# Attention followed by a gated MLP on one core: score visits in pairs over two PSUM tiles, the values of all heads in one tile, and a third PSUM bank for H

## The chip, the cores and the metric

The kernel runs on one core of one Trainium2 chip. The metric is the device time of one execution in microseconds (us); less is better. A core has a matmul engine (TensorE, PE in the profile, with its weight loads shown apart as PEld), a vector engine (DVE), an activation engine (ACT), GpSimd (POOL) and a queue engine (SP) that issues transfers. Matmuls write to PSUM, which has eight banks of 512 fp32 columns for each of 128 partitions; ACT and DVE read it.

## The reference

The inputs are q, k, v of 8 batches, 8 heads, 576 positions, 64 channels, and the weights of an MLP. Cut to what matters:

```python
scores = scale * q @ k.T                       # per batch and head, 576 x 576
rel = pos[:, None] - pos[None, :]
scores = where((rel >= 0) & (rel < 128), scores - slope[head] * abs(rel), -1e9)
attn = softmax(scores)                         # so each row sees at most 128 keys
x = (attn @ v)  as [8 * 576 tokens, 512]
h = x @ w_in                                   # 512 -> 2048
g = h * sigmoid(beta * h)
out = g @ w_out                                # 2048 -> 512, fp32
```

## The kernel before, in words

A batch has 5 blocks of queries (four of 128 rows, one of 64). Because of the window, a block of 128 keys is seen only by its own and the next block of queries. Scores are computed transposed: keys on the partitions, queries along the columns.

**Attention of batches 2 to 7.** A *score visit* is SC (L391): for one pair of heads p and one half m of a batch it makes 4 (m=0) or 6 (m=1) matmuls into the tile SS, which has two banks, one for each head of the pair. Each matmul contracts over 64 channels only, so it uses one half of the array's rows; the two heads of a pair (e = 0, 1) lie in the two halves. Then ACT takes Exp of all 1024 columns to the SBUF tile pt (L411), and DVE multiplies pt by the decay and the mask in one table (factor, L158 and L163). A batch has 4 pairs times 2 halves, 8 visits; batches 2 to 7 have 48. PV (L423) multiplies the weights of a block with v, for four heads g in one bank of the pool psum_t (two banks); a column of ones in v gives the sum of the weights. norm (L325) takes the reciprocal on DVE (L327) and multiplies (L328) into xn. Batches 0 and 1 have functions of their own (SP_, PVP, XP), which the change leaves as they are.

**Transposition.** X (L447) brings xn into XT, with the 512 channels on the partitions: for batches 2 and 3 with four TensorE transposes into a psum_t bank and a copy on DVE (L466); for batches 4 to 7 (XDMA = 4) with a transposing DMA from the SP queue (L455).

**MLP.** The 4608 tokens form nine groups g of 512 (NTG). Hm/HS (L475) makes one of 16 tiles of H: four matmuls of 512 columns into a bank of psum_h (two banks, named hps), then ACT takes Tanh (sig, L495; with half of beta, so that it serves as the sigmoid), then DVE makes gT from sig and hps (L496). OS (L505) makes a quarter n of an output tile i: four matmuls (L514) into a bank of psum_o (two banks, tag "ops"); after the last quarter the tile is halved to osb, by DVE for groups 0 and 1 (L522) and by ACT from group 2 on (L524), and stored. In groups 1 and 2 every second H tile up to a point (FOUR) also takes a bank of psum_o. The opening uses a tile SX of two banks; when it is closed, psum_o takes its place (open_o, L745).

**Loads.** q, k and v of the next batch come in blocks by DMAs of the SP queue (get, L188), are cast to bf16 on POOL (cast_qk, cast_v), and q and k are transposed by DMAs of the SP queue too (DT, L378).

**Order.** TensorE, SP and POOL keep the order in which the program lists the steps (manual_schedule, L598), each its own. The lists att (attention of batches 2 to 7) and items (H and O of a group) are merged: SC steps with the PV and X steps of the half before (merged, pvx, L547), the loads of batch b+1 at fixed places among the steps of batch b (jobs, L536), and spread (L715) puts the att steps between the items of a group by their weights, so that a group's tokens are ready before its first H. Each group g starts with H(g,0), needs the X blocks of its tokens, and ends with the output tiles O(g,0) and O(g,1), 32 matmuls without H between them; O(g,2) and O(g,3) fall among the H of the next group.

```python
for g in range(2, NTG):
    h = HG(g)
    o = (OG(g - 1, 2) if g > 2 else []) + OG(g - 1, 3)
    ...
    items += OG(g, 0) + OG(g, 1)
```

Of the kernel before, what the change touches and what calls it, by code (L numbers as in the profile page):

```python
# [19 lines left out]
def kernel(  # L20
# [62 lines left out]
    osb_pool = ctx.enter_context(tc.tile_pool(name="osb", bufs=4))  # L83
    psum_c = ctx.enter_context(tc.tile_pool(name="psum_c", bufs=1, space=bass.MemoryType.PSUM))
    psum_h = ctx.enter_context(tc.tile_pool(name="psum_h", bufs=2, space=bass.MemoryType.PSUM))
    psum_t = ctx.enter_context(tc.tile_pool(name="psum_t", bufs=2, space=bass.MemoryType.PSUM))
    SS = psum_c.tile([P, 2, 512], F32, name="SS")
    psum_c.seal()
    opening = ExitStack()
    psum_x = opening.enter_context(tc.tile_pool(name="psum_x", bufs=1, space=bass.MemoryType.PSUM))  # L90
    SX = psum_x.tile([P, 2, 512], F32, name="SX")
    late, gates = {}, {}

    def after(ins, other):
        tc.add_manual_dep(
# [219 lines left out]
    def room(b, shape):  # L315

        if b == 0:
            return psum_h.tile(shape, F32, name="pvh", tag="hps")[:]
        if "o" in late:
            return late["o"].tile(shape, F32, name="pvo", tag="ops")[:]  # L320
# [67 lines left out]

    COLS = {0: (0, 384), 1: (128, 256), 2: (0, 384), 3: (192, 320), 4: (128, None)}

    def SC(b, m, p):  # L391
        assert all((b, sb) in moved for sb in range((3, 5)[m]))
        qk = QK[b % 2]
        for kb in ((0, 1), (2, 4, 3))[m]:
            at, then = COLS[kb]
            nq = {3: P + 64, 4: 64}.get(kb, 2 * P)
            for e in range(2):
                o = SS[:, e, at : at + min(nq, 512 - at)]
                if kb in (0, 2):
                    o = bass.AP(  # L400
                        tensor=o.tensor, offset=o.offset,
                        ap=[list(o.ap[0]), [then - at, 2], [1, P]],
                    )
                nc.tensor.matmul(  # L404
                    o,
                    lhsT=qk[64 * e : 64 * e + 64, 1, p, P * kb : P * kb + P],
                    rhs=qk[64 * e : 64 * e + 64, 0, p, P * kb : P * kb + nq],
                    start=True, stop=True, skip_group_check=True,
                )
        pt = pt_pool.tile([P, 2, 512], BF16, name="pt", tag="pt")  # L410
        nc.scalar.activation(out=pt[:], in_=SS[:], func=ACTF.Exp, scale=qscale)  # L411
        factor(pt, m, p)
        pts[b, m, p] = pt

    def weights(b, kb, h, then):
        p, e = divmod(h, 2)
# [6 lines left out]
    def PV(b, qb, g):  # L423
        assert ("v", b, qb) in moved
        nq = ROWS[qb]
        vs = VS[b % 2]
        if g == 0:
            xns[b, qb] = xn_pool.tile([P, H, D], BF16, name="xn", tag="xn")
        xn = xns[b, qb]
        if b:  # L430
            pv = psum_t.tile([P, 4, 66], F32, name="pv", tag="t")
        else:
            pv = late["o"].tile([P, 4, 66], F32, name="pvo", tag="ops")
        for hl in range(4):
            h = 4 * g + hl
            if qb:
                nc.tensor.matmul(  # L437
                    pv[:, hl, 0 : D + 1], lhsT=weights(b, qb - 1, h, 1),
                    rhs=vs[:, qb - 1, h, 0 : D + 1], start=True, stop=False,
                )  # L440
            nc.tensor.matmul(  # L441
                pv[:, hl, 0 : D + 1], lhsT=weights(b, qb, h, 0),
                rhs=vs[:, qb, h, 0 : D + 1], start=qb == 0, stop=True,
            )
        norm(xn[0:nq, 4 * g : 4 * g + 4, :], pv, nq)

    def X(b, qb):  # L447
        nq = ROWS[qb]
        xnv = xns.pop((b, qb))[:].rearrange("p h d -> p (h d)")
        if b >= XDMA:  # L450
            tok0 = (b * S + P * qb) % XTR
            n1 = min(nq, XTR - tok0)
            for r0, r1, at in ((0, n1, tok0), (n1, nq, 0)):
                if r0 < r1:
                    nc.sync.dma_start(  # L455
                        out=XT[:, :, at : at + r1 - r0], in_=xnv[r0:r1], transpose=True)
            return
        xt = psum_t.tile([P, NDM, P], BF16, name="xt", tag="t")
        for c in range(NDM):
            nc.tensor.transpose(  # L460
                out=xt[:, c, 0:nq], in_=xnv[0:nq, c * P : (c + 1) * P],
                identity=ident[0:nq, 0:nq]
            )
        tok0 = (b * S + P * qb) % XTR
        n1 = min(nq, XTR - tok0)
        nc.vector.tensor_copy(out=XT[:, :, tok0 : tok0 + n1], in_=xt[:, :, 0:n1])  # L466
        if n1 < nq:
            nc.vector.tensor_copy(out=XT[:, :, 0 : nq - n1], in_=xt[:, :, n1:nq])
# [6 lines left out]
    def Hm(g, j, cs):  # L475
        if j == 0 and cs[0] == 0:
            gts[g] = gt_pool.tile([P, NFF, TOKG], BF16, name="gT", tag="gT")
        c0 = (g * TOKG) % XTR
        if cs[0] == 0:
            if g == 0 and j in (0, 3):  # L480
                hs[g, j] = SX[:, j // 2]
            elif j % 2 and j < FOUR.get(g, 0):
                hs[g, j] = late["o"].tile([P, DM], F32, name="hpo", tag="ops")[:]
            else:
                hs[g, j] = psum_h.tile([P, TOKG], F32, name="hps", tag="hps")[:]
        hps = hs[g, j]
        for c in cs:
            nc.tensor.matmul(  # L488
                hps, lhsT=W1[:, c, bass.ts(j, P)], rhs=XT[:, c, c0 : c0 + TOKG],
                start=(c == 0), stop=(c == NDM - 1),  # L490
            )
        if cs[-1] < NDM - 1:
            return
        sig = sig_pool.tile([P, TOKG], BF16, name="sig", tag="sig")
        gates[g, j] = nc.scalar.activation(out=sig[:], in_=hps, func=ACTF.Tanh, scale=beta_h[:, j : j + 1])  # L495
        gates["gT"] = nc.vector.scalar_tensor_tensor(  # L496
            out=gts[g][:, j, :], in0=sig[:], scalar=1.0, in1=hps, op0=ALU.add, op1=ALU.mult
        )
# [6 lines left out]
    def OS(g, i, n):  # L505
        gT = gts[g]
        if n == 0:
            late[g, i] = late["o"].tile([P, DM], F32, name="ops", tag="ops")
        ops_ = late[g, i][:]
        last = (g, i) == (NTG - 1, 3)  # L510
        for at in ((0, 256) if last else (0,)):
            cols = slice(at, at + 256) if last else slice(0, DM)
            for j in range(NFF) if last else range(4 * n, 4 * n + 4):
                nc.tensor.matmul(  # L514
                    ops_[:, cols], lhsT=gT[:, j, i * P : i * P + P], rhs=W2[:, j, cols],
                    start=(j == 0), stop=(j == NFF - 1),
                )
# [80 lines left out]
    with tc.manual_schedule(engines={ENG.PE, ENG.SP, ENG.Pool}):  # L598
# [157 lines left out]
        for f in steps:  # L756
# [58 lines left out]
```

## Time and profile before

| what | value |
|---|---|
| time, median of 8 runs | 331.97 us (331.13 to 334.83) |
| the profiled execution's own time | 331.97 us |
| its span (first to last instruction) | 330.2 us |
| granted TensorE clock | 1.00 |
| PE busy | 314.5 us (95%), 2252 matmuls in the records |
| DVE, ACT, POOL busy | 198.3 (60%), 186.6 (57%), 91.0 (28%) us |
| H matmuls L488 on hps | 131.7 us, 379 ns each |
| O matmuls L514 | 136.1 us, 373 ns each |
| Exp of a visit, L411 | x48, 1019 ns each |
| sig L495, gT L496 | 688 ns, 683 ns each |
| norm: reciprocal L327, product L328 | 173 ns, 420 ns each |
| chain that ended last | PE 81%, DMA 5%, DVE 4%, ACT 3%, SP queue 3% |

Busy times of matmuls overlap with each other in the records: a matmul of 512 columns is listed with 379 ns, while four of them start within 0.86 us. So distances are taken between starts. A few per cent of the matmul records are missing; a block of four then shows three. "issue" as a releaser means that nothing in the profile held the instruction back.

### The profile page before, as it was taken

The numbers are of one execution on the slowest core, as the hardware profiler recorded it, in microseconds if no ns is written. First come the engines' busy times: TensorE is split into PE (matmuls) and PEld (weight loads), VectorE is DVE, ScalarE is ACT, GpSimd is POOL, SyncE is SP. The second block draws the span as 40 slices with busy tenths as digits, with TensorE's granted clock in tenths as the row PEclk, the third lists the DMA queues.
The fourth block names the chain that finished last, engine by engine and source line by source line (L and its number), as shares of the span: only waits on it lengthen the run. The fifth ranks groups of instructions, "written<-read, shape, count | busy, mean of one in ns | idle before, by whom it ended". The sixth has DMA issues, their size and how long they took to land.

```text
span 330.2 us, 6005 instructions
## 1 busy us (share of the span) xinstructions
PE 314.5 (95%) x2252; PEld 150.3 (46%) x2294; DVE 198.3 (60%) x424; ACT 186.6 (57%) x265; POOL 91.0 (28%) x150
## 2 busy tenths in 40 slices
PE   7889979999999999999999999999999999999995
PEld 3454544443544454444444444444444445444443
DVE  6687777655669874866278627662877267334500
ACT  6858868615428744676466745664676465345511
POOL 4965811426544342443213221322000000000000
PEclk9999999999999999999999999999999999999999
DMA  7999999999999999999869896997022101210021
GB/s 216 251 256 248 178 197 216 198 191 209 248 186 254 198 205 235 205 187 217 189 124 211 167 231 131 203 190 151 18 64 57 64 16 50 58 64 33 4 94 64
DMA packets 147822, 51.80 MB, mean 157 GB/s; under 512 B 135360, under 2 KB 143824, under 8 KB 147792
## 3 DMA queue, kind: packets, MB, share of 16 engines
q1 hardware_dynamic: 139152, 38.29, 63.8%
q0 software_dynamic: 4864, 6.29, 9.6%
q10 hardware_dynamic: 3776, 6.83, 5.7%
q8 instruction: 18, 0.29, 0.4%
q14 instruction: 12, 0.10, 0.1%
HBM read 36.71 MB, written 9.44 MB: 140 GB/s over the span
## 4 chain that ended last, share of the span: by engine, by line
PE 81%; DMA 5%; DVE 4%; ACT 3%; SPq 3%; issue 2%; POOL 0%; ACTq 0%; DVEq 0%; POOLq 0%
PE ops L514 36%; PE hps L488 31%; DMA fst<-in_k_dram 5%; PE SS L404 4%; PE hpo L488 2%; SPq L205 2%; PE pv L441 2%; PE pv L437 2%; ACT pt L411 2%; DVE gT L496 1%; SPq L194 1%; PE xt L460 1%; ACT sig L495 1%; DVE pt L163 1%; ACT osb L524 1%
## 5 line engine op out<-in xcount | busy, mean ns | idle before, releaser
L514 PE MATMUL ops<-W,gT 128*128 128x512 bf16 (+1 forms) x574 | 136.1, 373 | 1.8 <-issue 0.6
L488 PE MATMUL hps<-XT,W 128*128 128x512 bf16 x511 | 131.7, 379 | 2.3 <-DVE gT L496 1.0
L496 DVE SCALAR_TENSOR_TENSOR gT<-sig,hps 128x512 bf16<-128x512 bf16 x133 | 90.2, 683 | 67.8 <-ACT sig L495 66.7
L495 ACT ACTIVATE sig<-hps,beta_h 128x512 bf16<-128x512 f32 x133 | 91.2, 688 | 61.4 <-PE hps L488 55.3
L514 PEld LDWEIGHTS <-gT 128*128 128x128 bf16 x592 | 54.1, 98 | 58.3 <-issue 3.0
L488 PEld LDWEIGHTS <-W 128*128 128x128 bf16 x576 | 50.5, 97 | 56.6 <-issue 7.1
L411 ACT ACTIVATE pt<-SS 128x1024 bf16<-128x1024 f32 x48 | 48.9, 1019 | 21.0 <-PE SS L404 21.0
L230 POOL CAST vs<-fst 128x512 bf16<-128x512 f32 (+1 forms) x40 | 26.9, 673 | 58.3 <-DMA fst<-in_v_dram 55.9
L524 ACT ACTIVATE osb<-ops 128x512 f32<-128x512 f32 (+1 forms) x28 | 16.5, 589 | 42.9 <-PE ops L514 42.9
L215 POOL CAST bst<-fst 128x512 bf16<-128x512 f32 (+1 forms) x32 | 20.6, 644 | 55.2 <-DMA fst<-in_q_dram 40.7
L328 DVE TENSOR_TENSOR xn<-pv,zs 128x256 bf16<-128x256 f32 (+1 forms) x62 | 26.0, 420 | 1.3
L216 POOL CAST bst<-fst 128x512 bf16<-128x512 f32 (+1 forms) x32 | 20.7, 647 | 19.5 <-DMA fst<-in_k_dram 19.4
L163 DVE TENSOR_TENSOR pt<-pt,fall 128x1024 bf16<-128x1024 bf16 x24 | 19.0, 790 | 10.3 <-ACT pt L411 10.2
L158 DVE TENSOR_TENSOR pt<-pt,falls 128x1024 bf16<-128x1024 bf16 x24 | 17.4, 723 | 12.6 <-ACT pt L411 12.5
L441 PE MATMUL pv<-vs,pt 128*128 128x65 bf16 x240 | 21.6, 193 | 0.0
L441 PEld LDWEIGHTS <-pt 128*128 128x128 bf16 x240 | 16.5, 97 | 8.4
L404 PE MATMUL SS<-qkT 64*128 64x256 bf16 (+2 forms) x240 | 18.9, 252 | 0.6
L437 PE MATMUL pv<-vs,pt 128*128 128x65 bf16 x192 | 18.1, 193 | 0.0
L437 PEld LDWEIGHTS <-pt 128*128 128x128 bf16 x192 | 15.2, 98 | 5.6
L522 DVE TENSOR_SCALAR osb<-ops 128x512 f32<-128x512 f32 (+1 forms) x9 | 5.9, 655 | 19.6 <-PE ops L514 19.6
L404 PEld LDWEIGHTS <-qkT 64*128 64x128 bf16 x240 | 8.0, 94 | 20.5 <-issue 18.6
L327 DVE RECIPROCAL zs<-pv 128x4 f32<-128x4 f32 (+1 forms) x67 | 11.1, 173 | 3.4 <-PE pv L441 2.8
(84 smaller groups left out, 180.6 us busy)
## 6 DMA issues: line engine op xcount, KB each, us to landing
fst<-in_k_dram SPq DMA_DIRECT2D x32, 256.0 KB, 5.4
fst<-in_q_dram SPq DMA_DIRECT2D x32, 256.0 KB, 5.3
fst<-in_v_dram SPq DMA_DIRECT2D x32, 256.0 KB, 4.7
out_dram<-osb ACTq DMA_DIRECT2D x26, 256.0 KB, 2.7
W<-in_moe_w_in_dram POOLq DMA_DIRECT2D x4, 512.0 KB, 7.9
W<-in_moe_w_out_dram POOLq DMA_DIRECT2D x4, 512.0 KB, 12.3
out_dram<-osb POOLq DMA_DIRECT2D x8, 256.0 KB, 4.0
fst<-in_q_dram SPq DMA_DIRECT2D x8, 128.0 KB, 3.9
```

The lines of the kernel that those rows point to most:

```text
L163: nc.vector.tensor_tensor(out=x, in0=x, in1=bass.AP(tensor=t.tensor, offset=t.offset, ap=[list(t.ap[0]), [P, 4], [0, 2], [1, P]]), op=ALU. ...
L216: return nc.gpsimd.tensor_copy(out=t[0:rows, 1], in_=fs.pop(("k", b, sb))[0:rows])
L230: return nc.gpsimd.tensor_copy(out=VS[b % 2][0:rows, sb, :, 0:D], in_=fs.pop(("v", b, sb))[0:rows])
L328: nc.vector.tensor_tensor(out=xn, in0=pv[0:nq, :, 0:D], in1=zs[0:nq].broadcast_to([nq, 4, D]), op=ALU.mult)
L404: nc.tensor.matmul(o, lhsT=qk[64 * e : 64 * e + 64, 1, p, P * kb : P * kb + P], rhs=qk[64 * e : 64 * e + 64, 0, p, P * kb : P * kb + nq], ...
L411: nc.scalar.activation(out=pt[:], in_=SS[:], func=ACTF.Exp, scale=qscale)
L437: nc.tensor.matmul(pv[:, hl, 0 : D + 1], lhsT=weights(b, qb - 1, h, 1), rhs=vs[:, qb - 1, h, 0 : D + 1], start=True, stop=False,)
L441: nc.tensor.matmul(pv[:, hl, 0 : D + 1], lhsT=weights(b, qb, h, 0), rhs=vs[:, qb, h, 0 : D + 1], start=qb == 0, stop=True,)
L488: nc.tensor.matmul(hps, lhsT=W1[:, c, bass.ts(j, P)], rhs=XT[:, c, c0 : c0 + TOKG], start=(c == 0), stop=(c == NDM - 1),)
L495: gates[g, j] = nc.scalar.activation(out=sig[:], in_=hps, func=ACTF.Tanh, scale=beta_h[:, j : j + 1])
L496: gates["gT"] = nc.vector.scalar_tensor_tensor(out=gts[g][:, j, :], in0=sig[:], scalar=1.0, in1=hps, op0=ALU.add, op1=ALU.mult)
L514: nc.tensor.matmul(ops_[:, cols], lhsT=gT[:, j, i * P : i * P + P], rhs=W2[:, j, cols], start=(j == 0), stop=(j == NFF - 1),)
```

## The change

- SC takes two pairs of heads: the matmuls of both come one after the other, the first pair's into one tile, the second's into another, then both Exp and both factors. The second tile is ST, two banks that psum_t held until X(1,4); psum_t is closed there (open_s).
- PV of batches 2 to 7 becomes PVB: one step for all 8 heads of a block, into the two banks of SS or ST, whichever was used longer ago (span), with one reciprocal and one product.
- X of batches 2 and 3 writes to SS or ST too, by matmuls with the identity instead of transposes, in fp32, and the copy to XT moves from DVE to ACT.
- psum_o has two tags of one bank each, "ops" and "h3". Up to group 1 output tiles and the H tiles of FOUR alternate between them. From group 2 on every third H tile (j % 3 == 2) takes "h3", output tiles take "ops", and output tile 0 of a group (and tile 2 of the last) takes a bank of psum_h.
- In att a pair of visits has twice the weight of a visit, PVB that of two PV. So steps stand in another order among the items.

The diff, without what is only renamed for it:

```diff
-    psum_t = ctx.enter_context(tc.tile_pool(name="psum_t", bufs=2, space=bass.MemoryType.PSUM))
+    trans = ExitStack()
+    psum_t = trans.enter_context(tc.tile_pool(side="right", name="psum_t", bufs=2, space=bass.MemoryType.PSUM))
...
+    spans = [SS]
+
+    def span():
+
+        spans.append(spans.pop(0))
+        return spans[-1]
+
+    def obank(name, tag=None):
+        if tag is None:
+            late["n"] = late.get("n", 0) + 1
+            tag = "ops" if late["n"] % 2 else "h3"
+        return late["o"].tile([P, DM], F32, name=name, tag=tag)[:]
...
-    def SC(b, m, p):
+    def SC(b, m, pp):
+
...
-        for kb in ((0, 1), (2, 4, 3))[m]:
-            at, then = COLS[kb]
-            nq = {3: P + 64, 4: 64}.get(kb, 2 * P)
-            for e in range(2):
-                o = SS[:, e, at : at + min(nq, 512 - at)]
...
+        spans.sort(key=lambda t: t is not SS)
+        for p, sps in zip(pp, spans):
+            for kb in ((0, 1), (2, 4, 3))[m]:
+                at, then = COLS[kb]
+                nq = {3: P + 64, 4: 64}.get(kb, 2 * P)
+                for e in range(2):
+                    o = sps[:, e, at : at + min(nq, 512 - at)]
...
-                nc.tensor.matmul(
-                    o,
-                    lhsT=qk[64 * e : 64 * e + 64, 1, p, P * kb : P * kb + P],
-                    rhs=qk[64 * e : 64 * e + 64, 0, p, P * kb : P * kb + nq],
...
-        pt = pt_pool.tile([P, 2, 512], BF16, name="pt", tag="pt")
-        nc.scalar.activation(out=pt[:], in_=SS[:], func=ACTF.Exp, scale=qscale)
-        factor(pt, m, p)
-        pts[b, m, p] = pt
+        for p, sps in zip(pp, spans):
+            pt = pt_pool.tile([P, 2, 512], BF16, name="pt", tag="pt")
+            nc.scalar.activation(out=pt[:], in_=sps[:], func=ACTF.Exp, scale=qscale)
+            factor(pt, m, p)
+            pts[b, m, p] = pt
...
-            pv = late["o"].tile([P, 4, 66], F32, name="pvo", tag="ops")
+            pv = room(1, [P, 4, 66])
...
+    def PVB(b, qb):
+
+        assert ("v", b, qb) in moved
+        nq = ROWS[qb]
+        vs = VS[b % 2]
+        xn = xns[b, qb] = xn_pool.tile([P, H, D], BF16, name="xn", tag="xn")
+        pv = span()[:, :, 0 : 4 * 66].rearrange("p g (h x) -> p g h x", x=66)
+        for h in range(H):
+            o = pv[:, h // 4, h % 4, 0 : D + 1]
+            if qb:
+                nc.tensor.matmul(
+                    o, lhsT=weights(b, qb - 1, h, 1), rhs=vs[:, qb - 1, h, 0 : D + 1],
+                    start=True, stop=False, skip_group_check=True)
+            nc.tensor.matmul(
+                o, lhsT=weights(b, qb, h, 0), rhs=vs[:, qb, h, 0 : D + 1],
+                start=qb == 0, stop=True, skip_group_check=True)
+        zs = xn_pool.tile([P, 2, 4, 1], F32, name="zb", tag="zb")
+        nc.vector.reciprocal(out=zs[0:nq], in_=pv[0:nq, :, :, D : D + 1])
+        nc.vector.tensor_tensor(
+            out=xn[0:nq].rearrange("p (g h) d -> p g h d", g=2), in0=pv[0:nq, :, :, 0:D],
+            in1=zs[0:nq].broadcast_to([nq, 2, 4, D]), op=ALU.mult)
...
+        tok0 = (b * S + P * qb) % XTR
+        n1 = min(nq, XTR - tok0)
+        if b >= 2:
+            xt = span()[:, 0, :].rearrange("p (c q) -> p c q", c=NDM)
+            for c in range(NDM):
+                nc.tensor.matmul(
+                    xt[:, c, 0:nq], lhsT=xnv[0:nq, c * P : (c + 1) * P], rhs=ident[0:nq, 0:nq],
+                    start=True, stop=True, skip_group_check=True)
+            nc.scalar.copy(out=XT[:, :, tok0 : tok0 + n1], in_=xt[:, :, 0:n1])
+            if n1 < nq:
+                nc.scalar.copy(out=XT[:, :, 0 : nq - n1], in_=xt[:, :, n1:nq])
+            return
...
-        tok0 = (b * S + P * qb) % XTR
-        n1 = min(nq, XTR - tok0)
...
             elif j % 2 and j < FOUR.get(g, 0):
-                hs[g, j] = late["o"].tile([P, DM], F32, name="hpo", tag="ops")[:]
+                hs[g, j] = obank("hpo", "h3" if j % 4 == 1 else "ops")
+            elif g > 1 and j % 3 == 2:
+                hs[g, j] = obank("hpo", "h3")
             else:
                 hs[g, j] = psum_h.tile([P, TOKG], F32, name="hps", tag="hps")[:]
...
         if n == 0:
-            late[g, i] = late["o"].tile([P, DM], F32, name="ops", tag="ops")
-        ops_ = late[g, i][:]
+            if g < 2:
+                late[g, i] = obank("ops", "h3" if i % 2 and (g, i) != (1, 3) else "ops")
+            elif i == 0 or i == 2 and g == NTG - 1:
+                late[g, i] = psum_h.tile([P, DM], F32, name="oph", tag="hps")[:]
+            else:
+                late[g, i] = obank("ops", "ops")
+        ops_ = late[g, i]
...
-            r += [(None, lambda g=g, qb=qb: PV(b, qb, g), 2) for g in range(2)]
+            r.append((None, lambda qb=qb: PVB(b, qb), 4))
...
-            a = [(None, lambda b=b, m=m, p=p: SC(b, m, p), w) for p in range(NP)]
+            a = [(None, lambda b=b, m=m, p=p: SC(b, m, (p, p + 1)), 2 * w) for p in (0, 2)]
...
-                tc.tile_pool(name="psum_o", bufs=2, space=bass.MemoryType.PSUM))
+                tc.tile_pool(name="psum_o", bufs=1, space=bass.MemoryType.PSUM))
...
+        def open_s():
+            trans.close()
+            psum_s = ctx.enter_context(
+                tc.tile_pool(name="psum_s", bufs=1, space=bass.MemoryType.PSUM))
+            spans.append(psum_s.tile([P, 2, 512], F32, name="ST"))
...
-                4: [lambda: PV(1, 4, 0), lambda: PV(1, 4, 1)], 5: [lambda: X(1, 4)]}
+                4: [lambda: PV(1, 4, 0), lambda: PV(1, 4, 1)], 5: [lambda: X(1, 4), open_s]}
```

More of the change, by code (lines that the diff above doesn't have):

```diff
@@ L319, in room @@
         if "o" in late:
-            return late["o"].tile(shape, F32, name="pvo", tag="ops")[:]
+            return obank("pvo")[:, 0 : 4 * 66].rearrange("p (h x) -> p h x", x=66)
         return psum_t.tile(shape, F32, name="pv", tag="t")[:]
@@ L389 @@
     COLS = {0: (0, 384), 1: (128, 256), 2: (0, 384), 3: (192, 320), 4: (128, None)}
-    def SC(b, m, p):
+    def SC(b, m, pp):
         assert all((b, sb) in moved for sb in range((3, 5)[m]))
         qk = QK[b % 2]
-        for kb in ((0, 1), (2, 4, 3))[m]:
-            at, then = COLS[kb]
-            nq = {3: P + 64, 4: 64}.get(kb, 2 * P)
-            for e in range(2):
-                o = SS[:, e, at : at + min(nq, 512 - at)]
[L399 to L402, printed above, removed]
-                    )
-                nc.tensor.matmul(
-                    o,
-                    lhsT=qk[64 * e : 64 * e + 64, 1, p, P * kb : P * kb + P],
-                    rhs=qk[64 * e : 64 * e + 64, 0, p, P * kb : P * kb + nq],
-                    start=True, stop=True, skip_group_check=True,
-                )
-        pt = pt_pool.tile([P, 2, 512], BF16, name="pt", tag="pt")
-        nc.scalar.activation(out=pt[:], in_=SS[:], func=ACTF.Exp, scale=qscale)
-        factor(pt, m, p)
-        pts[b, m, p] = pt
+        spans.sort(key=lambda t: t is not SS)
[5 more added lines that the diff above has]
+                    o = sps[:, e, at : at + min(nq, 512 - at)]
+                    if kb in (0, 2):
+                        o = bass.AP(
+                            tensor=o.tensor, offset=o.offset,
+                            ap=[list(o.ap[0]), [then - at, 2], [1, P]],
+                        )
+                    nc.tensor.matmul(
+                        o,
+                        lhsT=qk[64 * e : 64 * e + 64, 1, p, P * kb : P * kb + P],
+                        rhs=qk[64 * e : 64 * e + 64, 0, p, P * kb : P * kb + nq],
+                        start=True, stop=True, skip_group_check=True,
+                    )
+        for p, sps in zip(pp, spans):
[3 more added lines that the diff above has]
+            pts[b, m, p] = pt
     def weights(b, kb, h, then):
@@ L457, in X @@
             return
+        tok0 = (b * S + P * qb) % XTR
[3 more added lines that the diff above has]
+            for c in range(NDM):
+                nc.tensor.matmul(
+                    xt[:, c, 0:nq], lhsT=xnv[0:nq, c * P : (c + 1) * P], rhs=ident[0:nq, 0:nq],
[4 more added lines that the diff above has]
+            return
         xt = psum_t.tile([P, NDM, P], BF16, name="xt", tag="t")
```

## The prediction

> **What bounds the kernel now.** First the page's engine shares: TensorE (PE) is busy 95% of the span, no other engine over 60%, and the granted clock is full in every slice. Then the TensorE timeline of one stretch, to see what the 95% consists of:
>
> ```profile
> 160.47 1.03 PE L488 MATMUL hps<-XT,W 128*128 128x512 bf16 x4
> 161.42 0.39 PE L404 MATMUL SS<-qkT 64*128 64x256 bf16 x4
> 161.75 1.04 PE L488 MATMUL hps<-XT,W 128*128 128x512 bf16 x4
> 162.62 1.03 PE L514 MATMUL ops<-W,gT 128*128 128x512 bf16 x4
> ```
>
> Read starts, not durations (matmuls overlap). Four H matmuls take 162.62-161.75 = 0.87 us when an O block follows, 161.42-160.47 = 0.95 when a score visit follows: 0.08 more. The visit takes 161.75-161.42 = 0.33; its four matmuls run in pairs on two 64-row halves, so they stream for two times 256 columns, 2 x 0.108 = 0.22 (half of 0.87/4 each). 0.11 is left over. A visit thus pays **0.19 us** beyond its work, on entering and leaving 64-row matmuls. In the waits view the weight load of L404 is held back, by no semaphore, 44 times in 48 visits; its second line is X blocks (one transposition of a block each) right behind their values, its third H blocks that wait for gT.
>
> ```profile
> PEld L404 <- issue: 18.6, 44, 0.4
> PE xt L460 <- DVE xn L328: 1.4, 2, 0.8
> PE hps L488 <- DVE gT L496: 1.0, 4, 0.4
> ```
>
> The chain of work shows H blocks that came late because gT was late; an Exp or a factor stands ahead of it:
>
> ```profile
> 207.13 1.03 ACT pt L411
> 208.18 0.90 DVE pt L163
> 210.31 1.02 PE hps L488 x4
> ...
> 302.69 0.69 ACT sig L495
> 303.41 0.70 DVE gT L496
> 304.15 1.89 PE hps L488 x8
> ```
>
> By starts these waits on two hps banks are 0.31 (at 112.4), 0.33 (164.8), 0.61 (209.5), 0.14 (293.0), 0.43 (303.5). Last, the SP queue, which no busy share shows: its waits between 192 and 202 us, then its timeline with TensorE's:
>
> ```profile
> SPq L455 <- DVE xn L328: 5.1, 1, 5.1
> ```
>
> ```profile
> 201.21 1.21 SPq L455 DMA_TRANSPOSE XT<-xn  x1
> ...
> 215.67 2.67 SPq L382 DMA_TRANSPOSE qkT<-bst  x1
> 218.43 1.19 SPq L455 DMA_TRANSPOSE XT<-xn  x1
> ...
> 222.58 1.89 SPq L455 DMA_TRANSPOSE XT<-xn  x1
> ...
> 226.93 1.02 PE L488 MATMUL hps<-XT,W 128*128 128x512 bf16 x4
> ```
>
> SP stands 5.1 us before X(5,2) (the DMA that transposes batch 5, block 2, L455) until its values are normalized, then issues without a pause: 17 loads and transposes, up to X(6,0) at 222.58. That one lands 4.2 us later, 226.8; group 6's first H begins at 226.93, 0.35 instead of 0.22 after the last O matmul. So the end of group 5 hangs on **SP, not TensorE**. Group 4 likewise: X(4,2) leaves at 166.68, X(5,1) at 189.84 lands 3.4 later, 193.2; H(5,0) begins at 194.24, 1.0 us of slack.
>
> **What the Trainium skill says.** "TensorEngine Tiling (Array Packing)", Key Properties: "Changing tiling mode (not just tile) drains the TensorE". The trace agrees: 0.08 + 0.11 per visit; it gives no figure. "PSUM — Partial Sum Buffer", PSUM bank collisions: engines must be kept apart per bank, so a matmul into SS or ST waits for its last reader; in the trace the third visit of batch 2 starts at 78.28, right after the Exp at 77.20 (1.03 long). "Perfetto Trace Analysis", What "DMA-bound" means: an issuing engine whose track is solid DMA slices is itself the bound; SP between 201.2 and 224.5 is that. "DMA: Bandwidth & Descriptors", Anatomy of one DMA: semaphore waits are done by the issuing sequencer, so a waiting X holds the loads behind it (5.1 us above).
>
> **The change, part by part.** Sums are against the profiled execution (331.97 us, span 330.2, 1.8 around it; it equals the median of the eight runs).
>
> *Pairs of visits.* 48 visits become 24 pairs: 24 x 0.19 = **-4.6 us** of TensorE. 12 fall before H(4,0) (-2.3), 7 in groups 4 and 5 (-1.3), 4 in group 6 (-0.8), 1 in group 7 (-0.2). Not hidden: TensorE has no idle time around visits.
>
> *Second tile ST.* Visits 3 and 4 of batch 2 stood behind the Exp of the visit before, with one O block between: starts at 77.75 and 81.41 show 0.21 each. With two tiles and more O between: -0.4.
>
> *One tile for all heads.* Values of 8 heads take 16 x 0.030 either way: 0. Normalizing becomes 1 reciprocal and one 512-wide product instead of 2 x (0.17+0.42) = 1.2; from 256 to 512 fp32 elements the nearest row is the 0.68 of L522, so 0.17+0.69 = 0.86: DVE saves some 10 us, worth nothing there (60% busy). But it starts only after all 16 matmuls. X(2,2) before the change waits 0.79 right behind its values; now one O (0.86) lies between against 0.2 + 0.86 + 0.1 = 1.2: 0.3 remains, and X(3,2), which was covered, gets 0.3: -0.5 + 0.3.
>
> *X of batches 2 and 3* goes from a transpose and DVE copy to a matmul and ACT copy: same 4 x 0.056 on TensorE; ACT +10 x 0.59 (row L355), DVE -10 x 0.41; ACT is near 70% busy there, bound 0 to +0.6 (one copy late once); I take 0 because at least one O lies between.
>
> *Third bank for H.* Every third H of groups 2 to 8 goes to bank h3. Each bank is reused after three H instead of two: -0.31 before H(4,0), -0.33 and -0.61 in groups 4 and 5, -0.57 in group 8. From group 2 on O keeps "ops" alone (and a hps bank for one tile of each group); between the end of one O tile and the next on "ops" lie at least two H (1.73) against 0.2 + 0.6 + up to 0.7 behind a sigmoid: 0. O keeps two banks up to group 1. One collision: in group 2 H(2,1) and H(2,2) both take h3, with only a pair between. H(2,2) waits for gT: 1.06 + 0.72 + 0.69 + 0.07 = 2.54 after H(2,1)'s start (H at 131.50, its sigmoid at 132.56, gT at 133.28, each lasting 0.69), and TensorE would be there at 0.86 + 0.62 = 1.48: **+1.1**. Behind it the whole queue waits. SC(3,0), in the same place, needs the transpose issued at 90.89, landing 5.7 later at 96.6; before the change it was used at 96.73. TensorE now comes about 0.8 earlier and POOL's fourth store stands ahead of the first cast of batch 3 (up to +0.6): a wait of up to 1.2, under the same shadow as gT, so not added.
>
> Sum up to H(4,0): -2.3 - 0.4 - 0.2 - 0.3 + 1.1 = **-2.1**.
>
> *What is late next: X(4,2) and X(5,2).* Order on TensorE in group 4 was H, visit, H, O, values, H, values; it is H, H, pair, O, H, H, all values. A pair takes 0.19 + 4 x 0.108 = 0.62. The last values end 5.40 after the group's start (4 H and one O 4.32, pair 0.62, values 0.46) instead of 164.84-160.47 = 4.37. ACT runs both Exp (2 x 1.02) ahead of the next two sigmoids: Exp 2.6 to 4.7, sigmoids to 6.1; DVE then does factor, gT, reciprocal, gT, product to 7.6. X(4,2) leaves at 7.65 instead of 166.68-160.47 = 6.2: +1.45. In group 5 likewise 8.2 instead of 6.97: +1.2. Behind each stand the same 19 and 17 issues; X(4,4) and X(5,4) move ahead of one load and one transpose, but their values are ready by then (about 16 after the start, SP comes there at 21): 0. H(5,0) then cannot start before 7.65 + 26.6 + 0.1 = 34.35 into group 4 (26.6 = 193.25-166.68), was 33.77; H(6,0) not before 8.2 + 25.6 + 0.1 = 33.9 into group 5, was 32.69. Together 0.55 + 1.2 = **+1.75**; the 1.3 of drains and 0.94 of gT waits saved there buy nothing.
>
> After H(6,0) the loads are over and TensorE bounds again: -0.8 - 0.2 - 0.57 = **-1.6**.
>
> Total: -2.1 + 1.75 - 1.6 = -1.95: **330.0 us** (own range 328.8 to 331.4). POOL's later stores and casts change places too; the casts wait for loads there (55.9 us for v in the waits view), so that costs 0.
>
> **Rivals.**
> *The SP chain gives way* (transposes of 1.2 to 2.7 us shorten, or X leaves earlier): groups 4 and 5 keep their -1.3 - 0.94 - 0.1 too: -2.1 - 2.35 - 1.6 = -6.05, **325.9**. For it: transposes of 1.2 exist. Against: 0.13 us of waiting for X(6,0) already before.
> *Slower: SS and ST passed around.* Scores, values and X share two tiles; in before, values had two banks of their own. Place: the value or X block after each of 24 pairs. TensorE comes there at 0.62 + 2 x 0.86 = 2.3 after the pair's start; SS is free at about 0.9 (one sigmoid first) + 1.02 = 1.9, or 2.6 with two sigmoids ahead; ST at 3.0 to 3.6. A wait of 0.3 per pair eats 7 us: **335**; it decides from a mean of 0.08 per pair (no gain), 0.15 (slower by 0.5%). Against: ST comes second, after 0.46 + 0.86 more.
> *It doesn't do what it says*: the drain belongs to each visit's own bank change. The -3.3 outside groups 4 and 5 fall away: **333.3**.
>
> **Chances.** Forecast 0.57, chain gives way 0.23, shared tiles 0.13, drain stays 0.07. A measurement of this kernel can tell about 0.5% (1.66 us) from no change. Of the forecast, 330.3 divides faster from same: 0.34 to 0.23. Faster 0.34 + 0.23 = 0.57, rounded 0.58; same 0.23 + 0.07 = 0.30, less rounding 0.29; slower 0.13. The range covers forecast and first rival (0.80): 325.8 to 332.2.
>
> **What would show it.** Pair to next start about 0.62 with eight matmuls; no hps wait on gT but one of 1 us at H(2,2); H(5,0) and H(6,0) right after an X landing, with TensorE idle 1 to 2.5 us before them; X(4,2) some 7.6 after group 4's start. Wrong if SP pauses inside its runs, if TensorE is idle behind pairs at L477 or L502, or if O waits on "ops".

## The result, and the profile after

The changed kernel takes 333.57 us (median of 21 runs, 331.28 to 336.98), the kernel before beside it 331.74 us (median of 58 runs). The ratio of the times is **1.0045**, 95% interval 1.003 to 1.0059: slower by some 0.45%. The ratio counts fast executions alone, so it gives 1.5 us where the two medians are 1.8 apart. The forecast of 330.0 us was wrong in sign, and the time lies outside its range (325.8 to 332.2). The profiled execution of the changed kernel has a span of 332.1 us (its own time 333.89), that of before 330.2 us: 1.9 us more, and these 1.9 us are followed here.

In the changed kernel SC is at L420, PVB at L474 and L477, its reciprocal and product at L481 and L482, X of batches 2 and 3 at L502 (matmul) and L505 (copy), X by DMA at L494, transposes of q and k (DT) at L395, H at L539, gT at L547, O at L570, the factor at L171 and L176.

First, where the time lies. The starts of H(g,0) on TensorE's timeline cut the span into stretches (us):

| stretch | before | predicted change | after | measured change |
|---|---|---|---|---|
| start to H(4,0) | 160.47 | -2.1 | 160.14 | -0.33 |
| group 4 | 33.78 | +0.55 | 34.38 | +0.60 |
| group 5 | 32.69 | +1.2 | 34.62 | +1.93 |
| group 6 | 33.27 | -0.8 | 33.78 | +0.51 |
| group 7 | 30.44 | -0.2 | 30.21 | -0.23 |
| group 8 to the end | 39.55 | -0.57 | 38.99 | -0.56 |

Three stretches came out as forecast. Three did not: the one up to H(4,0), group 5 and group 6. The -0.33 up to H(4,0) holds +0.29 that is there when the first pair begins (74.90; before the change the first visit began at 74.61), and which differs from one execution to the next: the kernels of the first and third experiments below begin theirs at 74.95 and 74.52. From the first visit on the change gained 0.62.

The waits view of the changed kernel (in total, times, longest):

```profile
PEld L420 <- issue: 11.3, 25, 0.9
...
PE hps L539 <- DMA XT<-xn: 5.0, 2, 3.2
...
PE hpo L539 <- DVE gT L547: 1.0, 1, 1.0
...
PE SS L420 <- DVE xn L482: 0.9, 1, 0.9
```

Weight loads of score matmuls are now held back 25 times, not 44. Of the four waits of H for gT in this view one is left, that of H(2,2). New are two waits of H for transposed X, 5.0 us together, and one of scores for a *product*.

A pair on TensorE's timeline:

```profile
196.25 1.03 PE L570 MATMUL ops<-W,gT 128*128 128x512 bf16 x4
197.21 0.39 PE L420 MATMUL SS<-qkT 64*128 64x256 bf16 x4
197.44 0.38 PE L420 MATMUL ST<-qkT 64*128 64x256 bf16 x4
197.75 1.04 PE L539 MATMUL hpo<-XT,W 128*128 128x512 bf16 x4
```

By starts, four O matmuls take 0.96 ahead of the pair (0.86 elsewhere), and both visits together 0.54. The second visit starts 0.23 after the first: nothing is lost between them. The pair ahead of H(2,2), with the one wait for gT that is left:

```profile
97.80 0.39 PE L420 MATMUL SS<-qkT 64*128 64x256 bf16 x4
98.03 0.38 PE L420 MATMUL ST<-qkT 64*128 64x256 bf16 x4
99.42 1.89 PE L539 MATMUL hpo<-XT,W 128*128 128x512 bf16 x8 [1.01 <-DVE gT L547]
```

Here H(2,2) starts 1.39 after the second visit, where 0.31 passes in the pair above: a wait of 1.08.

The stretch up to H(4,0), on the timelines of POOL, DVE and TensorE of the changed kernel:

```profile
82.08 0.54 POOL L588 DMA_DIRECT2D out_dram<-osb  x1 [2.63 <-DVE osb L578]
82.62 0.62 POOL L228 CAST bst<-fst 128x512 bf16<-128x512 f32 x1
82.87 4.28 DVE L171 TENSOR_TENSOR pt<-pt,falls 128x1024 bf16<-128x1024 bf16 x2 [0.49 <-ACT pt L428]
...
85.40 0.60 POOL L229 CAST bst<-fst 128x512 bf16<-128x512 f32 x1
...
87.31 0.69 DVE L482 TENSOR_TENSOR xn<-SS,zb 128x512 bf16<-128x512 f32 x1
...
88.05 0.40 PE L420 MATMUL SS<-qkT 64*128 64x256 bf16 x6 [0.89 <-DVE xn L482]
88.89 0.40 PE L420 MATMUL ST<-qkT 64*128 64x256 bf16 x6 [0.44 <-DVE xn L482]
```

POOL's fourth store waited 2.63 us for its osb, and the six casts of batch 3 behind it then ran without a gap, 82.62 to 86.0. In that time DVE had two factors to do. They took 4.28 us: 3.68 for the first, 0.68 for the second, which ran after the casts. So DVE came to the values of SS at 87.08, though TensorE had finished them at about 84; the next scores waited for SS, then for ST.

The same place before the change:

```profile
81.92 1.20 DVE L163 TENSOR_TENSOR pt<-pt,fall 128x1024 bf16<-128x1024 bf16 x1 [0.48 <-ACT pt L411]
...
83.54 0.54 POOL L532 DMA_DIRECT2D out_dram<-osb  x1
84.08 0.62 POOL L215 CAST bst<-fst 128x512 bf16<-128x512 f32 x1
...
85.74 0.61 POOL L216 CAST bst<-fst 128x512 bf16<-128x512 f32 x1
...
86.71 0.69 DVE L158 TENSOR_TENSOR pt<-pt,falls 128x1024 bf16<-128x1024 bf16 x1
```

The fourth store stood between the second and the third cast. Four casts ran in a row here too, from 84.08 to 86.35, but no factor fell into that time; the products of the normalization that did took their usual 0.42.

The ends of groups 4 (first line) and 5, on the timelines of SP and TensorE, and the granted clock on the page:

```profile
194.51 1.90 PE L539 MATMUL hps<-XT,W 128*128 128x512 bf16 x8 [1.79 <-DMA XT<-xn]
...
224.40 1.37 SPq L494 DMA_TRANSPOSE XT<-xn  x1
...
229.13 3.24 PE L539 MATMUL hps<-XT,W 128*128 128x512 bf16 x8 [3.16 <-DMA XT<-xn]
232.31 0.40 PE L420 MATMUL SS<-qkT 64*128 64x256 bf16 x6
```

```profile
PEclk9999999999999999999999999997999999999999
```

X(6,0) left SP at 224.40 and landed at 228.89; TensorE stood idle for 3.16 us. Then eight H matmuls took 232.31 - 229.13 = 3.18 us. Eight ahead of a pair take 1.82 where TensorE was busy before (229.63 - 227.81 in the third experiment below). Six of the starts here follow each other at 0.42 to 0.43, elsewhere at 0.216: half the rate, and one slice of the clock row shows 7 for 9. Before the change no slice did. Taken closely, the granted clock is 0.50 from 228.50 to 231.91. At H(5,0), after 1.79 us of idling, it stayed at 1.00.

### The profile page after: what moved, and what is told of

Same layout as the page of the kernel before. It is cut to its first block, busy times and chain, and to the rows that moved or that the text cites. A ratio compares the mean times of both kernels' runs of the same rounds, so it can differ in the third digit from the quotient of the medians.

```text
span 332.1 us, 5973 instructions
## 1 busy us (share of the span) xinstructions
PE 310.9 (94%) x2251; PEld 153.2 (46%) x2294; DVE 194.0 (58%) x354; ACT 189.5 (57%) x275; POOL 89.3 (27%) x150
## 4 chain that ended last, share of the span: by engine, by line
PE 77%; DVE 8%; DMA 5%; ACT 5%; issue 2%; SPq 1%; POOL 1%; DVEq 0%; ACTq 0%; POOLq 0%
PE ops L570 24%; PE hps L539 23%; PE hpo L539 11%; PE oph L570 7%; DMA XT<-xn 2%; DVE gT L547 2%; PE SS L420 2%; DMA fst<-in_k_dram 2%; DVE pt L171 2%; ACT pt L428 1%; PE ST L420 1%; ACT sig L546 1%; PE SS L477 1%; PE SS L474 1%; DMA fst<-in_v_dram 1%
## 5 line engine op out<-in xcount | busy, mean ns | idle before, releaser
L547 DVE SCALAR_TENSOR_TENSOR gT<-sig,hps 128x512 bf16<-128x512 bf16 x99 | 67.2, 684 | 71.7 <-ACT sig L546 70.6
L570 PE MATMUL ops<-W,gT 128*128 128x512 bf16 (+1 forms) x450 | 107.7, 372 | 1.2 <-ACT osb L580 0.5
L539 PE MATMUL hps<-XT,W 128*128 128x512 bf16 x381 | 99.6, 384 | 5.7 <-DMA XT<-xn 5.0
L546 ACT ACTIVATE sig<-hps,beta_h 128x512 bf16<-128x512 f32 x99 | 68.0, 690 | 48.6 <-PE hps L539 46.3
L539 PEld LDWEIGHTS <-W 128*128 128x128 bf16 x576 | 53.2, 98 | 68.3 <-issue 10.0
L570 PEld LDWEIGHTS <-gT 128*128 128x128 bf16 x592 | 55.5, 98 | 60.9 <-issue 1.9
L539 PE MATMUL hpo<-XT,W 128*128 128x512 bf16 x167 | 43.4, 379 | 1.2 <-DVE gT L547 1.0
L546 ACT ACTIVATE sig<-hpo,beta_h 128x512 bf16<-128x512 f32 x43 | 29.6, 689 | 15.6 <-PE hpo L539 13.0
L547 DVE SCALAR_TENSOR_TENSOR gT<-sig,hpo 128x512 bf16<-128x512 bf16 x43 | 29.5, 685 | 14.0 <-ACT sig L546 13.8
L428 ACT ACTIVATE pt<-SS 128x1024 bf16<-128x1024 f32 x24 | 24.4, 1017 | 13.1 <-PE SS L420 13.1
L570 PE MATMUL oph<-W,gT 128*128 128x512 bf16 x121 | 28.7, 379 | 0.3
L428 ACT ACTIVATE pt<-ST 128x1024 bf16<-128x1024 f32 x24 | 24.6, 1024 | 0.0
L176 DVE TENSOR_TENSOR pt<-pt,fall 128x1024 bf16<-128x1024 bf16 x24 | 18.5, 779 | 9.8 <-ACT pt L428 9.7
L171 DVE TENSOR_TENSOR pt<-pt,falls 128x1024 bf16<-128x1024 bf16 x24 | 20.0, 838 | 5.0 <-ACT pt L428 5.0
L477 PEld LDWEIGHTS <-pt 128*128 128x128 bf16 x240 | 14.8, 97 | 4.2
L474 PEld LDWEIGHTS <-pt 128*128 128x128 bf16 x192 | 13.4, 97 | 2.8
```

What stands on the lines that cost most here:

```text
L171: nc.vector.tensor_tensor(out=pt[:], in0=pt[:], in1=falls[:, 2 * p : 2 * p + 2], op=ALU.mult)
L176: nc.vector.tensor_tensor(out=x, in0=x, in1=bass.AP(tensor=t.tensor, offset=t.offset, ap=[list(t.ap[0]), [P, 4], [0, 2], [1, P]]), op=ALU. ...
L428: nc.scalar.activation(out=pt[:], in_=sps[:], func=ACTF.Exp, scale=qscale)
L474: nc.tensor.matmul(o, lhsT=weights(b, qb - 1, h, 1), rhs=vs[:, qb - 1, h, 0 : D + 1], start=True, stop=False, skip_group_check=True)
L477: nc.tensor.matmul(o, lhsT=weights(b, qb, h, 0), rhs=vs[:, qb, h, 0 : D + 1], start=qb == 0, stop=True, skip_group_check=True)
L539: nc.tensor.matmul(hps, lhsT=W1[:, c, bass.ts(j, P)], rhs=XT[:, c, c0 : c0 + TOKG], start=(c == 0), stop=(c == NDM - 1),)
```

## Experiments

Ratios are to the kernel before, run beside it on the same chip. All kernels compute the whole result; where matmuls on zeros are put in, their output is overwritten.

**The transposing DMA of block 2 one place later.** The edit, in pvx:

```diff
-                r.append(((b, qb), lambda qb=qb: X(b, qb), 0))
+                for x in {2: (), 3: (2, 3)}.get(qb, (qb,)):
+                    r.append(((b, x), lambda x=x: X(b, x), 0))
```

> The changed kernel, with the transposing DMA of block 2 of batches 4 to 7 listed together with that of block 3, so that SP does not stand 5 us or more in front of it. Theory (SP starts its loads too late, TensorE idles 1.95 us before H(5,0) and 3.3 us before H(6,0), and runs at half clock behind the second): all three go, 1.95 - 0.2 + 3.3 - 0.3 + 1.5 = 6.3 us less than the changed kernel, about 327. Rival A (the chain of loads is as long as the time of the group whatever SP does first, or the values of blocks 3 then hold it): the waits stay, within 1 us of the changed kernel. Rival B (only the SP wait of one of the two groups was the cause): 2 to 4 us less.

327.32 us, ratio **0.987** (0.9846 to 0.9894). Against the changed kernel that is 333.57 - 327.32 = 6.25 us less (5.8 by the ratios), as the theory said. What the edit does on SP is less than its words: X(b,2) moves past one pair of loads, and SP still stands before it. SP in the changed kernel:

```profile
158.71 1.07 SPq L207 DMA_DIRECT2D fst<-in_k_dram  x1
167.34 1.21 SPq L494 DMA_TRANSPOSE XT<-xn  x1
```

and in this one:

```profile
159.71 2.66 SPq L207 DMA_DIRECT2D fst<-in_q_dram  x1
162.41 1.41 SPq L207 DMA_DIRECT2D fst<-in_k_dram  x1
167.39 1.22 SPq L494 DMA_TRANSPOSE XT<-xn  x1
168.71 1.24 SPq L395 DMA_TRANSPOSE qkT<-bst  x1
```

X(4,2) leaves at the same time, but a pair of loads that stood behind it is now issued while SP waits, and a transpose of q and k is next. X(5,1) follows 20.3 us later (187.74), not 23.4 (190.78). H(5,0) and H(6,0) do not wait any more; groups 4, 5 and 6 take 32.42, 31.28 and 32.42. These are 1.36, 1.41 and 0.85 less than before the change.

**The same move in the kernel before.** The edit is the same.

> The kernel before, with the same move of the transposing DMA of block 2 of batches 4 to 7 behind the values of block 3. Theory (before the change TensorE bounded, and SP's wait cost 0.13 us ahead of H(6,0)): 0.1 to 0.3 us less than the kernel before. Rival (the move is worth the same whatever the score visits do): 5 us less.

331.73 us, ratio 1.0003 (0.9989 to 1.0017). So the move is worth nothing while TensorE is the bound, and 6 us once the visits are paired: the loss was not an old one that nobody had removed, but one that the change made.

**TensorE kept busy during the wait for X(6,0).**

```diff
+            if g == 6:
+                idle(12)
             items = []
```

> The changed kernel with twelve matmuls on zeros put ahead of H(6,0), written to a score tile that is overwritten later; they keep TensorE busy during the wait for X(6,0). Theory (the eight H matmuls at 427 ns behind that wait are a lower clock, granted after 3.3 us of idling): H(6,0) starts at the same time within 0.2, the next starts follow at 216 ns, 1.5 us less than the changed kernel, about 332.0. Rival (the 427 ns come from something else than the idling, such as PSUM or a DMA): no change, 333.5 or later.

331.69 us, ratio 1.000 (0.9976 to 1.0025); 1.0045 - 1.000 is 1.5 us. TensorE's timeline:

```profile
224.81 2.32 PE L118 MATMUL SS<-zeros 128*128 128x512 bf16 x10
227.81 1.89 PE L539 MATMUL hps<-XT,W 128*128 128x512 bf16 x8 [0.69 <-DMA XT<-xn]
229.63 0.40 PE L420 MATMUL SS<-qkT 64*128 64x256 bf16 x6
```

The matmuls on zeros shorten the idle time to 0.69, and the eight H matmuls take 1.82 by starts where they took 3.18. Group 5 is as long as before this edit (34.74; 34.62), group 6 is 32.42, not 33.78: 1.36 less. The half rate came from the idling.

The other executions say the same, and more. Of 22 of the changed kernel five had a mean granted clock of 0.998 or more, and took 330.8 to 332.2 us; the other 17 had 0.995 or less and took 332.4 us or more. With the matmuls on zeros 12 of 14 had 0.999 or more. So the half rate seems to come in most executions of the changed kernel, not in all (a low mean can also come from the opening, as the last section shows), and in the five without it the kernel is about as fast as the kernel before: medians of 331.6 and 331.7.

Group 4 was shorter by 1.05 in this trace as well, on the same list of instructions: where SP bounds, the stretch differs by that much between these two executions.

**Four casts of batch 3 on ACT**, so that POOL has no run of six:

```diff
+        if b == 3 and sb in (1, 2):
+            nc.scalar.copy(out=t[0:rows, 0], in_=fs.pop(("q", b, sb))[0:rows])
+            return nc.scalar.copy(out=t[0:rows, 1], in_=fs.pop(("k", b, sb))[0:rows])
```

> The changed kernel with the casts of q and k of blocks 1 and 2 of batch 3 on ACT, in place of POOL, so that no run of six casts stands on POOL. Theory (the factor that begins at 82.87 takes 3.68 us because POOL casts without a pause beside it, and PVB's tile stays taken for that long): the factor takes 1.3 us or less, the waits of 1.0 and 0.5 us of the scores of SC(2,1:(2,3)) on the product go; H(4,0) starts 1.5 us earlier. As groups 4 and 5 hang on SP and its wait for values that TensorE makes, all of it reaches the end: 1.5 us less than the changed kernel. Rival (DVE is late for another reason): factor as long as before, 0; the four casts on ACT (0.6 us each) delay Exp and sig, +0.5.

331.31 us, ratio 0.9982 (0.9968 to 0.9997): 2.1 us less than the changed kernel's 1.0045. DVE and TensorE:

```profile
82.94 2.07 DVE L171 TENSOR_TENSOR pt<-pt,falls 128x1024 bf16<-128x1024 bf16 x2 [0.49 <-ACT pt L431]
...
98.54 0.29 PE L423 MATMUL SS<-qkT 64*128 64x256 bf16 x2 [1.87 <-DMA qkT<-bst]
```

The two factors take 2.07 instead of 4.28 (1.47 beside the two casts that POOL still does, 0.68 without any), and both waits for a product are gone. The cause of the long factor is shown. But H(4,0) comes only 0.32 earlier (159.82): TensorE now reaches SC(3,0) at 96.4, and the transposed q and k of batch 3, block 2, land at 98.50. The H(2,2) wait lies in that shadow and is gone too. What the time gained came from groups 4 and 5 in the trace (32.98 and 34.11), within the variation seen in the run before; why they were shorter is not settled. That the median came down by the 1.5 us that the theory forecast, and more, is therefore luck.

**H(2,2) on hps**, together with the moved DMA:

```diff
-            elif g > 1 and j % 3 == 2:
+            elif g > 1 and j % 3 == 2 and (g, j) != (2, 2):
```

> The kernel with the transposing DMA of block 2 moved (327.3 us), and H(2,2) on a bank of hps, so that it does not wait for the gT of H(2,1) on h3. Theory (a wait of 0.8 to 1.1 us that TensorE does not make up): 0.8 to 1.1 us less than 327.3. Rival (the bank of hps is taken as long, or the scores of batch 3 wait for their transposes instead): 0.

327.05 us, ratio 0.9865 (0.985 to 0.9881): the same as without it. TensorE's timeline:

```profile
98.32 0.28 PE L420 MATMUL SS<-qkT 64*128 64x256 bf16 x2
99.11 0.28 PE L420 MATMUL SS<-qkT 64*128 64x256 bf16 x2 [0.50 <-DMA qkT<-bst]
```

H(2,2) waits no more; SC(3,0) waits for the same transpose, which landed at 99.07 here (at 98.15 in the trace without this edit, where SC(3,0) waited 0.2 for it). Group 2 is shorter by 0.21 only. The rival held.

**Single visits on SS and ST, with the moved DMA.**

```diff
-        spans.sort(key=lambda t: t is not SS)
-        for p, sps in zip(pp, spans):
+        mine = [span() for _ in pp]
+        for p, sps in zip(pp, mine):
...
-            a = [(None, lambda b=b, m=m, p=p: SC(b, m, (p, p + 1)), 2 * w) for p in (0, 2)]
+            a = [(None, lambda b=b, m=m, p=p: SC(b, m, (p,)), w) for p in range(NP)]
```

> The kernel with the transposing DMA of block 2 moved (327.3 us), but with the 48 visits one by one at half the weight each, on SS and ST in turn with the values. Theory (TensorE bounds, and pairs are worth 24 x 0.19 us): 4.6 us more than 327.3. Rival A (the gain over the kernel before lies in the order, the joined values and the third bank): within 1 us of 327.3. Rival B (visits alone free their tiles later for the values): more than 7 us more.

332.06 us, ratio 1.002 (1.001 to 1.003): 332.06 - 327.32 = **4.7 us** more. The pairs are worth what the drains were priced at, and all else in the change (values in one tile, X on ACT, the third bank) is worth nothing on balance: this kernel has it all and takes 0.2% longer than the kernel before. In its trace groups 4, 5 and 8 are 0.5, 0.8 and 0.55 shorter than before, and H(4,0) is 1.8 later (162.25), with H(2,2) waiting 1.8 for its gT. So the 4.7 are not drains alone: 2.06 of them lie ahead of H(4,0), where that wait is 1.0 longer than with pairs (idle for 1.78 and 0.77) and other waits differ too. From H(4,0) to the last output tile TensorE waits for nothing in either trace; there the 12 pairs save 2.56 us, **0.21 us** each.

**One more 128-row matmul between the visits of each pair, or ahead of it**, with the moved DMA:

```diff
         for p, sps in zip(pp, spans):
+            if p == pp[1]:
+                nc.tensor.matmul(
+                    sps[:, 0, 0:64], lhsT=zeros[:, 0:P], rhs=zeros[:, 0:64], start=True,
+                    stop=True, skip_group_check=True)
```

(pp[0] in the second kernel.)

> The kernel with the transposing DMA of block 2 moved (327.3 us), and in each of the 24 pairs of visits one more matmul, over all 128 rows, 64 columns of zeros, between the two visits; its output is overwritten at once. Theory (TensorE drains 0.19 us per excursion into 64-row matmuls): 24 x (0.19 + 0.03 for the columns) = 5.3 us more, and 24 x 0.19 = 4.6 more than the next kernel, which has the same matmuls in another place. Rival (the loss of a visit came from something else, such as the change of PSUM tile): 24 x 0.03 = 0.7 more, and the same time as the next kernel.

> As the kernel before this one in the list, but the additional 128-row matmul of each pair stands ahead of the pair, where TensorE is in 128-row matmuls anyway. Theory (only changes between 64-row and 128-row matmuls drain): 24 x 0.03 = 0.7 us more than 327.3. Rival (any matmul put in costs what the other costs): as much as with the matmul between the visits.

332.19 us (ratio 1.0018, 1.0004 to 1.0032) and 328.07 us (0.9893, 0.9878 to 0.9908), against 327.32 with neither. The same 24 matmuls cost 4.9 us between the visits and 0.75 ahead of them; (332.19 - 328.07) / 24 = **0.17 us** for leaving and entering 64-row matmuls once. From H(4,0) on, where TensorE does not wait, the trace with the matmul between is 2.93 us longer than the one with neither: 0.24 for each of 12 pairs, 0.21 without the 0.03 of the matmul itself. TensorE's timeline with the matmul between:

```profile
172.66 0.39 PE L424 MATMUL SS<-qkT 64*128 64x256 bf16 x4
172.99 0.20 PE L411 MATMUL ST<-zeros 128*128 128x64 bf16 x1
173.12 0.39 PE L424 MATMUL ST<-qkT 64*128 64x256 bf16 x4
173.45 1.04 PE L543 MATMUL hps<-XT,W 128*128 128x512 bf16 x4
```

The second visit starts 0.46 after the first instead of 0.23: 0.33 for the first visit with its exit, and 0.13 for the matmul of 64 columns with the re-entry.

**The edits together.** Moved DMA, H(2,2) on hps and the four casts on ACT; and the same with the transposes of blocks 1 and 2 of batch 3 ahead of the loads of q, k of block 4 and the first v:

```diff
-            r.append((2 * sb + 4, lambda sb=sb: cast_qk(b, sb)))
-            r.append((2 * sb + 6, lambda sb=sb: DT(b, sb)))
+            early = b == 3 and sb in (1, 2)
+            r.append((5 + sb if early else 2 * sb + 4, lambda sb=sb: cast_qk(b, sb)))
+            r.append((6.5 + sb / 2 if early else 2 * sb + 6, lambda sb=sb: DT(b, sb)))
```

> Three edits together: the transposing DMA of block 2 moved (327.3 us alone), H(2,2) on hps, and the casts of q and k of blocks 1 and 2 of batch 3 on ACT. Theory (each of the last two alone uncovers the wait for the transposed q and k of batch 3, which land at about 98.5 whatever TensorE does): SC(3,0) waits some 2 us, and the time is within 0.7 us of 327.3, about 326.9. Rival (the waits of 1.4 and 1.07 us are independent and both come off): 324.8.

> As the kernel before this one in the list, and the transposes of blocks 1 and 2 of batch 3 are issued ahead of the loads of q, k of block 4 and of the first v. Theory (the late transpose of block 2, issued at 90.7 and landing at 98.5, is what SC(3,0) waits for): the transpose lands before 96.3, the wait goes, and both savings are left over: 324.8 to 325.2 us. Rival (transfers already under way hold the transpose up, not its place on SP; or block 4 comes too late instead): as the kernel before it.

325.55 us (ratio 0.9813, 0.9782 to 0.9843) and **325.24 us** (0.9805, 0.9777 to 0.9833). In the first, SC(3,0) waited 0.63 and not 2 us: the transpose landed at 97.12, not at the 98.5 that the theory took as fixed. That time falls between the two expectations. In the second it was issued at 88.42 and landed at 91.63, and TensorE runs through the place:

```profile
96.15 0.39 PE L423 MATMUL SS<-qkT 64*128 64x256 bf16 x4
96.38 0.38 PE L423 MATMUL ST<-qkT 64*128 64x256 bf16 x4
96.69 1.04 PE L542 MATMUL hps<-XT,W 128*128 128x512 bf16 x4
```

The span is 323.3; H(4,0) starts at 157.93, 2.5 us ahead of the kernel before. The two medians do not differ by more than their intervals; what the place of the transpose is worth beyond the trace is open. Both kernels beat the kernel before and the changed one, by 6 and 8 us.

## Why the prediction was wrong, step by step

- *Pairs, -4.6 us.* **Right.** 4.7 by single visits, 4.1 by the matmul between; 0.21 for each pair where TensorE waits for nothing else, priced at 0.19. The rival that the drain belongs to each visit's bank change (333.3) came near the time by accident, and its mechanism is refuted: with another tile and no change of rows the second visit starts at once.
- *Second tile and X, -0.4 and -0.2.* Nearly. The waits behind visits of batch 2 are gone; X(2,2) and X(3,2) wait 0.40 each where 0.3 was said. That costs 0.2.
- *Third bank.* **Right.** The gT waits are gone, and H(2,2) waits 1.08 (said: 1.1). The wait of up to 1.2 for SC(3,0)'s transpose did not come in this trace: the transpose landed at 96.43, and TensorE, held up before, reached SC(3,0) at 97.80 only. It came in the runs in which TensorE was there sooner or the transpose later, and took the gain when H(2,2) was mended.
- *"POOL's fourth store stands ahead of the first cast"*, counted as at most 0.6 for SC(3,0) and then nothing. **This step failed first.** The store waited for DVE, the six casts behind it met a factor on DVE, and the factor of 0.68 took 3.68. By starts TensorE waited 0.96 for SS and 0.61 for ST, 1.57 us that the sum had at nothing. With the 0.2 above this makes the -2.1 a -0.33, and -0.33 was measured; that the numbers are equal is luck, since the measured one holds the 0.29 from before the first pair, and the 12 drains ahead of H(4,0) are worth some 0.2 more than said if they too cost 0.21. POOL's work was only asked for who waits for it, not for what it does to the engine beside it. The Trainium skill has it in "SBUF — State Buffer", Who interferes with whom: a DVE instruction with two SBUF inputs contends with a GpSimd instruction that reads SBUF, and one of the two blocks. The traces agree: 1.2 us was the longest factor there before the change, beside two casts; 1.47 beside two casts with four on ACT, 3.68 beside six.
- *X(4,2) and X(5,2).* **Right, with one size off.** X(4,2) left 7.21 us into group 4 (said: 7.65), X(5,2) 7.93 into group 5 (8.2), and group 4 took 34.38 (34.35). In group 5 the chain from there to the landing of X(6,0) took 26.45 us, not the 25.6 copied from before; with X(5,2) 0.27 earlier than said, group 5 ended 0.7 late. Group 4 of the changed kernel was 34.38 and 33.33 in two traces of the same instructions there, so the term deserved a range of 1 us.
- *After H(6,0), -1.6.* **This step failed too.** Groups 7 and 8 came out as said, group 6 lost 1.36 to the clock. The idle time before H(6,0) was forecast, but its price was taken as its length. "TensorE: Matmul & The Clock Gate", What's actually happening, names an idle window of about 3.4 us after which TensorE runs at half rate, and says that the window runs freely, so its start is not that of the idling. Here 3.16 us of idling was enough, and 2.65 in the kernel with casts on ACT; 1.79 before H(5,0) was not. In both traces the clock stayed at 0.50 for 3.41 us. That five executions of the changed kernel escaped it agrees with a window that runs freely; how long TensorE stood idle in those is not on record. Without the idling, group 6 is 0.85 shorter than before, as forecast (0.8).
- *The slow rival*, SS and ST passed around, at 0.3 per pair: not so. (Its sum does not come out either: 330.0 and 7 make 337, not 335.) Behind pairs only X(2,2) and X(3,2) wait, 0.8 us in all. What waits for the tiles is the next scores, once, because DVE was held up.
- *The first rival*, the SP chain giving way at 325.9, is what the moved DMA makes. It reaches 327.3, since up to H(4,0) the two waits stay.

In sum, by the stretches: 1.77 up to H(4,0), 0.05 in group 4, 0.73 in group 5 and 1.31 in group 6 more than said, 3.9 together, from -1.95 to +1.9. Of what the change gained on TensorE, 4.6 us, nothing was left: SP's order of issues, one run of casts and the clock behind an idle engine took it. The first of these was forecast; the other two are the steps that failed.

## What to carry to other kernels

Fewer entries into half-height matmuls are worth a fifth of a microsecond each here, but only where TensorE is the bound; so when a step is moved later, follow the transfer that waits for it, and let loads that need nothing go ahead of that transfer. Idle time of TensorE can cost more than its length: 2.65 and 3.16 us of it brought 1.4 to 1.6 us on top here, though, it seems, not in every execution. And ask of a moved run of casts not only who waits for it, but which DVE instructions now run beside it.

## What the runs showed of the hardware that was not expected

- A DVE product of two bf16 tiles in SBUF, 128 x 1024, takes 0.68 us alone, 1.1 to 1.5 beside two POOL casts of 128 x 512 in a row, and 3.5 to 3.7 beside six (six traces): it is held for the whole run, not for one cast. These casts keep their 0.55 us distance. A cast can be held too: before the change one that began during a factor took 1.12 (82.47), not 0.62.
- After 2.65 and 3.16 us without matmuls, the next matmuls of 512 columns start 0.43 us apart until the 3.41 us at a granted clock of 0.50 are over, then 0.216 again; after 1.79 us they do not. One long idle stretch is not needed: in three traces (single visits, and the last two kernels) the clock is 0.50 from 7.9 to 11.3 us as well, in the opening, where TensorE idled three times for 0.35 to 0.51 us in the 3.4 us before, by the records.
- The transposing DMA of batch 3, block 2 landed 5.7 to 7.8 us after its issue behind three loads of 256 KB (90.89 to 96.59 before the change, 90.68 to 98.50 in the kernel with casts on ACT), and 3.2 us after it when it was issued ahead of them (88.42 to 91.63). The spread is between executions with the same list of issues there. That the loads were the cause was not tried by itself.
